# Two 1 KB loads moved from ScalarE's DMA queue into SyncE's, behind the first weight

## The chip, the cores and the metric

The kernel runs on one core of a Trainium2 chip. The metric is the device time of one execution in microseconds (us). Times of a kernel are given as the median of several runs; one further execution is recorded by the hardware profiler, and every duration of a single instruction or transfer below comes from that one.

## The reference

One token is decoded. `x` is a single row of 512 values. It is normalised, and two branches read the result; the output adds their product to `x`:

```
xn = layernorm(x)
s  = attention(xn)      # 32 heads, the last 4096 of 32768 cached keys and values, head size 128
g  = silu(mlp(xn))      # layernorm, w1, shift by one token, w2, residual, layernorm, w3, gelu, w4
out = x + s * g
```

Each head has its own keys and values. Per head the window is 4096 x 128 in bf16, 1 MB of keys and 1 MB of values, so 64 MB of cache are read once. `wq` (512 x 4096) and `wo` (4096 x 512) are 4 MB each, the weights of the second branch 3.2 MB (`w1` isn't loaded, because with one token the shift by a token leaves zeros before `w2`). Each byte is used about once: the kernel mostly moves memory.

## The kernel before

**Loads.** All large loads go through one helper, `load` (L77-78), which issues them from SyncE (SP) in the order of the program. In that order: `w2_sb` (512 KB, L86), `w3_sb` (1376 KB, L88), `w4_sb` in three pieces (L90-92), `wq_sb` (4096 KB, L94), then, from the loop at L525 on, tiles of keys and values (`kv`, 2048 KB each for two heads). The profile names the first three tiles all `w_sb`. Two loads of 1 KB don't use the helper and are issued from ScalarE (ACT): `x_bf` (L81), which lays `x` out as 128 partitions x 4 values, so 128 runs of 8 bytes, and `x_row` (L84), which puts it as four rows of 128 values on partitions 0, 32, 64 and 96 of a tile that GpSimd has cleared at L83.

**Who reads x.** `x_f` (L180) copies `x_bf` to float32. From it comes the front chain: the statistics of the first layernorm (`ln_stats`, L155-176), `xn_bf`, the second layernorm with `w2`, the products with `w3` (L212) and `w4` (L223), `g_row` (L233), then the queries: `qT_ps` (L239), `q_rows` (L246) and `q_bc` (L253), which holds each pair's query on all partitions. `x_row` is read by `xn_row` (L203) and by the last addition (L614).

**The loop.** For each of 16 pairs of heads, part of the keys is multiplied with `q_bc` on VectorE (DVE) and summed (L313, L315), the rest is transposed on TensorE, copied by ACT (L329) and multiplied with the query on TensorE (L334). Softmax is done per four heads, values are applied three pairs later (`LAG`, L442 and L431), and the result goes through `wo`.

**What orders the loads.** SP waits before an issue until the buffer is free and until an earlier load that used the same completion semaphore has landed; there are eight such semaphores for the loads of SP and ACT, used in turn. Keys have six buffers (`K_BUFS`). The first four tiles of keys are issued right behind `wq_sb`. The buffers of the values lie where the weights were: the pool of weights is closed at L529-530, so the first tile of values is issued only when the last reader of the weights' pool, the products from `q_rows` at L251, is done:

```python
        kn = load_kv(k_pool, A_k_cache, s) if s < NP else None
        if s == LAG:
            wts_guard.__exit__(None, None, None)
            v_pool = ctx.enter_context(tc.tile_pool(name="v", bufs=V_BUFS))
```

The engines' own order in the loop is the order of the program (a manual schedule, L521).

Of the kernel before, what the change touches and what calls it, by code (L numbers as in the profile page):

```python
# [8 lines left out]
P = 128  # L9
# [20 lines left out]
def kernel(  # L30
# [14 lines left out]
    nc = tc.nc  # L45
# [10 lines left out]
    KC = D // P  # L56
# [20 lines left out]
    def load(dst, src):  # L77
        return tc.keep_in_program_order(nc.sync.dma_start(out=dst, in_=src))  # L78

    x_bf = small.tile([P, KC], BF16, name="x_bf")  # L80
    nc.scalar.dma_start(out=x_bf[:], in_=A_x.rearrange("a b (p c) -> p (a b c)", p=P))  # L81
    x_row = small.tile([P, P], BF16, name="x_row")
    nc.gpsimd.memset(x_row[:], 0.0)  # L83
    nc.scalar.dma_start(out=x_row[0:P:32, :], in_=A_x.rearrange("a b (j n) -> (a b j) n", j=KC))  # L84
    w2_sb = wts.tile([P, KC, D], BF16, name="w2_sb")
    load(w2_sb[:], B_w2.rearrange("(p c) n -> p c n", p=P))  # L86
    w3_sb = wts.tile([P, KC, F], BF16, name="w3_sb")
    load(w3_sb[:], B_w3.rearrange("(p c) n -> p c n", p=P))  # L88
    w4_sb = wts.tile([P, 11, D], BF16, name="w4_sb")
# [171 lines left out]
    for c in range(2):  # L261
        nc.vector.tensor_copy(
            out=few[:, c, 0:4 * NE].rearrange("p (a b) -> p a b", b=4),
            in_=ident_bf[:, 4 * NE * c:4 * NE * (c + 1)].rearrange("p (b a) -> p a b", b=4))
# [27 lines left out]
    for r in range(2):  # L292
        nc.vector.tensor_copy(out=pick_f[:, :, r, :],
                              in_=ident_bf[:, 32 * r:32 * r + 8].rearrange("p (i a) -> p i a", a=2))
# [351 lines left out]
```

## Time and profile before

| what | value |
|---|---|
| median of 5 runs | 196.59 us |
| the five runs | 195.49, 195.68, 196.59, 196.65, 196.74 us |
| the profiled execution, its own time | 195.39 us |
| span of its instructions | 193.5 us |
| bytes loaded | 78.84 MB |
| busy: DVE, PE, ACT | 145.3, 135.9, 78.9 us |

The profile is of one execution. Its span begins with the first and ends with the last recorded instruction; the 1.9 us between span and time lie outside. The page gives busy times of the engines, and the same in 40 equal slices of 4.84 us, with the share of time in which the core's 16 DMA engines were busy and the rate at which they moved bytes. A DMA is issued by an engine's sequencer (SPq, ACTq), split into packets, put into rings of the 16 DMA engines, and lands some time later. A row of the timeline gives start, duration, engine and line of an instruction; a row of the windows gives the work of each engine, the DMA share and the rate in a stretch of time. The page's queue q1 is SP's, q10 is ACT's.

### The profile page before, as it was taken

The numbers are of one execution on the slowest core, as the hardware profiler recorded it, in microseconds if no ns is written. First come the engines' busy times: TensorE is split into PE (matmuls) and PEld (weight loads), VectorE is DVE, ScalarE is ACT, GpSimd is POOL, SyncE is SP. The second block draws the span as 40 slices with busy tenths as digits, with TensorE's granted clock in tenths as the row PEclk, the third lists the DMA queues.
The fourth block names the chain that finished last, engine by engine and source line by source line (L and its number), as shares of the span: only waits on it lengthen the run. The fifth ranks groups of instructions, "written<-read, shape, count | busy, mean of one in ns | idle before, by whom it ended". The sixth has DMA issues, their size and how long they took to land.

```text
span 193.5 us, 4727 instructions
## 1 busy us (share of the span) xinstructions
PE 135.9 (70%) x2108; PEld 104.8 (54%) x2108; DVE 145.3 (75%) x164; ACT 78.9 (41%) x173; POOL 6.3 (3%) x13
## 2 busy tenths in 40 slices
PE   0549779673785999397979976456757897857751
PEld 0444468573784945235978352146747556845640
DVE  1550119999999999999999999199999987792001
ACT  2003019871945742327468053161545047733000
POOL 2210007000000000000000000000000000000000
PEclk9999966967558559759655596995556697585555
DMA  5999999999999999999999999999999999999980
GB/s 211 404 490 433 389 423 430 428 427 433 430 427 427 423 422 423 430 433 433 430 433 420 423 433 430 430 430 430 430 430 430 430 422 435 417 433 420 410 315 5
DMA packets 7051, 79.13 MB, mean 409 GB/s; under 512 B 888, under 2 KB 1752, under 8 KB 2264
## 3 DMA queue, kind: packets, MB, share of 16 engines
q1 hardware_dynamic: 6880, 78.84, 96.0%
q8 instruction: 16, 0.26, 0.5%
q10 hardware_dynamic: 152, 0.00, 0.0%
q14 instruction: 3, 0.02, 0.0%
HBM read 78.84 MB, written 0.00 MB: 407 GB/s over the span
## 4 chain that ended last, share of the span: by engine, by line
DMA 41%; DVE 38%; PE 10%; issue 4%; SPq 3%; ACT 2%; POOL 1%; DVEq 0%; POOLq 0%
DMA kv<-in_A_k_cache_dram 31%; DVE S L315 23%; DVE prod L313 12%; DMA wo_rows<-in_A_wo_dram 7%; SPq L78 3%; DMA x_bf<-in_A_x_dram 2%; ACT kt L329 2%; PE qT_ps L239 2%; PE oT L442 2%; PE hr_ps L223 2%; PE a_ps L212 1%; PE hr_ps L220 1%; PE oT L449 1%; PE pt L328 1%; DVE m L353 1%
## 5 line engine op out<-in xcount | busy, mean ns | idle before, releaser
L315 DVE TENSOR_REDUCE S<-prod 128x20 f32<-128x2560 bf16 (+1 forms) x32 | 83.8, 2620 | 1.1
L329 ACT COPY kt<-pt 128x1024 bf16<-128x1024 bf16 x54 | 51.0, 1022 | 27.9 <-PE pt L328 27.9
L313 DVE TENSOR_TENSOR prod<-kv,q_bc 128x2560 bf16<-128x2560 bf16 (+1 forms) x32 | 44.3, 1385 | 9.2 <-DMA kv<-in_A_k_cache_dram 6.7
L328 PE MATMUL pt<-ident_bf,kv 128*128 128x128 bf16 x432 | 40.9, 277 | 10.1 <-DMA kv<-in_A_k_cache_dram 8.4
L328 PEld LDWEIGHTS <-kv 128*128 128x128 bf16 x432 | 37.3, 129 | 13.4 <-DMA kv<-in_A_k_cache_dram 9.4
L334 PE MATMUL sT<-qT_bf,kt 128*128 128x2 bf16 x432 | 17.6, 165 | 12.2 <-ACT kt L329 11.8
L442 PE MATMUL oT<-pT,kv 128*128 128x2 bf16 x768 | 22.3, 165 | 4.3 <-DMA kv<-in_A_v_cache_dram 4.3
L442 PEld LDWEIGHTS <-kv 128*128 128x128 bf16 x768 | 21.4, 102 | 5.7 <-DMA kv<-in_A_v_cache_dram 5.6
L334 PEld LDWEIGHTS <-kt 128*128 128x128 bf16 x432 | 15.6, 101 | 15.1 <-ACT kt L329 14.4
L431 PE MATMUL ov<-kv,pT 128*8 128x512 bf16 x64 | 21.9, 519 | 0.0
L431 PEld LDWEIGHTS <-pT 128*8 128x8 bf16 x64 | 6.7, 109 | 14.2 <-issue 11.5
L371 PE MATMUL mb_ps<-md,par_t 4*128 4x4 f32 x16 | 4.5, 349 | 10.1 <-DVE md L363 10.1
L378 ACT ACTIVATE pT<-S,mb 128x64 bf16<-128x64 f32 x32 | 10.9, 356 | 0.2
L371 PEld LDWEIGHTS mb_ps<-md,par_t 4*128 4x128 f32 x16 | 4.0, 306 | 10.7 <-issue 9.5
L374 ACT COPY mb<-mb_ps 128x4 f32<-128x4 f32 x8 | 1.3, 162 | 20.6 <-PE mb_ps L371 20.6
L462 DVE TENSOR_TENSOR o<-oT,rden 128x2 bf16<-128x2 f32 x3 | 0.5, 160 | 10.8 <-PE oT L442 10.8
L466 ACT ACTIVATE o<-oT,rden 128x1 bf16<-128x1 f32 x26 | 4.7, 264 | 6.3 <-PE oT L449 4.2
L226 DVE COPY hr<-hr_ps 1x512 f32<-1x512 f32 x1 | 0.7, 679 | 7.7 <-PE hr_ps L223 7.7
L378 ACT ACTIVATION_READ_ACCUMULATOR pT<-S,mb 128x1 f32 x32 | 6.0, 187 | 0.0
L157 PE MATMUL ln_ps<-x_f,ones_f 128*128 128x4 f32 x4 | 1.2, 366 | 5.8 <-DVE x_f L180 4.8
L215 ACT ACTIVATE a_bf<-a_ps 128x10 bf16<-128x10 f32 x1 | 0.2, 179 | 12.1 <-PE a_ps L212 12.1
L507 PE MATMUL yr_ps<-wo,ox 128*1 128x512 bf16 x16 | 5.0, 483 | 0.0
(116 smaller groups left out, 93.6 us busy)
## 6 DMA issues: line engine op xcount, KB each, us to landing
kv<-in_A_k_cache_dram SPq DMA_DIRECT2D x16, 2048.0 KB, 29.7
kv<-in_A_v_cache_dram SPq DMA_DIRECT2D x15, 2048.0 KB, 26.6
wq_sb<-in_A_wq_dram SPq DMA_DIRECT2D x1, 4096.0 KB, 17.8
wo<-in_A_wo_dram SPq DMA_DIRECT2D x1, 2048.0 KB, 27.1
w_sb<-in_B_w_dram SPq DMA_DIRECT2D x1, 1376.0 KB, 6.8
w_sb<-in_B_w_dram SPq DMA_DIRECT2D x1, 1024.0 KB
wo<-in_A_wo_dram SPq DMA_DIRECT2D x1, 1024.0 KB, 26.9
kv<-in_A_v_cache_dram SPq DMA_DIRECT2D x1, 1024.0 KB
```

What stands on the lines that cost most here:

```text
L78: return tc.keep_in_program_order(nc.sync.dma_start(out=dst, in_=src))
L313: nc.vector.tensor_tensor(out=prod[:, 0:m, :], in0=kn[:, rows, :], in1=q_bc[:, s:s + 1, :].to_broadcast([P, m, Dh]), op=ALU.mult)
L315: nc.vector.tensor_reduce(out=st[s // 2]["S"][:, s % 2, rows], in_=prod[:, 0:m, :], axis=AX.X, op=ALU.add)
L328: nc.tensor.transpose(pt[:, i, :], kn[:, n + b + i, :], ident_bf[:])
L329: nc.scalar.copy(out=kts[s][:, b:b + w, :], in_=pt[:, 0:w, :])
L334: nc.tensor.matmul(st[s // 2]["sT"][:, s % 2, c, :], lhsT=kt[:, c, :], rhs=qT_bf[:, 2 * s:2 * s + 2], start=True, stop=True)
L371: nc.tensor.matmul(mb_ps[:], lhsT=par_t[:].rearrange("k b a -> k (b a)"), rhs=md[:].rearrange("k r a -> k (r a)"), start=True, stop=True)
L378: nc.scalar.activation(out=s["pT"][:, i // 2, :, i % 2], in_=s["S"][:, i // 2, :], func=ACT.Exp, scale=scale, bias=mb[:, i:i + 1], accum_o ...
L431: nc.tensor.matmul(s["ov"][32 * r:32 * r + 8], lhsT=s["pT"][:, r, c:c + 4, :].rearrange("p i a -> p (i a)"), rhs=v[:, c:c + 4, :], start=F ...
L442: nc.tensor.matmul(s["oT"][:, 2 * r:2 * r + 2], lhsT=v[:, c, :], rhs=s["pT"][:, r, c, :], start=(c == 0), stop=(c == CP - 1))
L466: nc.scalar.mul(o_blk[b][:, c + k:c + k + 1], st[g]["oT"][:, hl + k:hl + k + 1], st[g]["rden"][:, hl + k:hl + k + 1])
L507: nc.tensor.matmul(yr_ps[:], lhsT=ox_blk[i][:, t:t + 1], rhs=wo_blk[i][:, t, :], start=(t == 0), stop=(t == n - 1))
```

## The change

Both loads of `x` are issued through `load`, so from SP, after `w2_sb` and ahead of `w3_sb`. The clearing of `x_row` on GpSimd stays where it was. Nothing else is edited.

```diff
     x_bf = small.tile([P, KC], BF16, name="x_bf")
-    nc.scalar.dma_start(out=x_bf[:], in_=A_x.rearrange("a b (p c) -> p (a b c)", p=P))
     x_row = small.tile([P, P], BF16, name="x_row")
     nc.gpsimd.memset(x_row[:], 0.0)
-    nc.scalar.dma_start(out=x_row[0:P:32, :], in_=A_x.rearrange("a b (j n) -> (a b j) n", j=KC))
     w2_sb = wts.tile([P, KC, D], BF16, name="w2_sb")
     load(w2_sb[:], B_w2.rearrange("(p c) n -> p c n", p=P))
+    load(x_bf[:], A_x.rearrange("a b (p c) -> p (a b c)", p=P))
+    load(x_row[0:P:32, :], A_x.rearrange("a b (j n) -> (a b j) n", j=KC))
     w3_sb = wts.tile([P, KC, F], BF16, name="w3_sb")
     load(w3_sb[:], B_w3.rearrange("(p c) n -> p c n", p=P))
```

## The prediction

> **What bounds the kernel now.** I read the page's slices and its table of queues first.
>
> ```profile
> span 193.5 us, 4727 instructions
> ...
> DMA  5999999999999999999999999999999999999980
> GB/s 211 404 490 433 389 423 430 428 427 433 430 427 427 423 422 423 430 433 433 430 433 420 423 433 430 430 430 430 430 430 430 430 422 435 417 433 420 410 315 5
> ...
> q1 hardware_dynamic: 6880, 78.84, 96.0%
> ...
> q10 hardware_dynamic: 152, 0.00, 0.0%
> ```
>
> From the second slice to the 38th the 16 DMA engines are busy nine tenths or more, at about 430 GB/s. SP's queue holds 96.0% of the engines' time. 78.84 MB at 430 GB/s are 183.4 us of the 193.5; the other 10 us are the start (nothing moves before 1.5 us, and the first slice runs at 211 GB/s) and the tail behind the last data. DVE with 145.3 us is not the bound. The chain of waits names keys with 31% and DVE with 35%, but its pieces of keys are transfers that wait in a full queue: one issued at 94.76 takes 31.37 us for 2 MB, which alone would be 4.9 us. So the time is: when the stream starts, plus 183 us, plus gaps, plus the tail. A change to two 1 KB loads can act on the start, or by letting the stream run dry later.
>
> The start, in the windows (us, five engines' busy time with counts, PE clock, DMA share, GB/s):
>
> ```profile
> 1.50:1.75 0.25, 0.00 (x0) 0.00 (x0) 0.00 (x0) 0.00 (x0) 0.25 (x2) 1.00 0.05 16
> 1.75:2.00 0.25, 0.00 (x0) 0.00 (x0) 0.00 (x0) 0.00 (x0) 0.04 (x1) 1.00 1.10 246
> 2.00:2.25 0.25, 0.00 (x0) 0.00 (x0) 0.00 (x0) 0.00 (x0) 0.00 (x0) 1.00 0.46 82
> 2.25:2.50 0.25, 0.00 (x0) 0.00 (x0) 0.00 (x0) 0.22 (x1) 0.00 (x0) 1.00 0.37 98
> 2.50:2.75 0.25, 0.00 (x0) 0.00 (x0) 0.00 (x0) 0.25 (x1) 0.00 (x0) 1.00 0.28 115
> 2.75:3.00 0.25, 0.00 (x0) 0.00 (x0) 0.00 (x0) 0.25 (x1) 0.00 (x0) 1.00 0.58 230
> 3.00:3.25 0.25, 0.00 (x0) 0.00 (x0) 0.00 (x0) 0.25 (x1) 0.00 (x0) 1.00 1.10 410
> ```
>
> The first packets of `w2_sb` move at about 1.6 us, then the engines are half empty until 2.9 us. The packet records show `w2_sb` (4096-byte packets) from 1.60 to 3.84 us, the 8-byte packets of `x_bf` between them from 2.58 to 3.86, the first of `w3_sb` (11008 bytes) at 3.63, and the four 256-byte packets of `x_row` only at 5.49 to 5.92.
>
> Then the timeline of the issues:
>
> ```profile
> 0.73 0.41 ACTq L81 DMA_DIRECT2D x_bf<-in_A_x_dram  x1
> ...
> 1.18 1.07 ACTq L84 DMA_DIRECT2D x_row<-in_A_x_dram  x1
> ...
> 3.25 0.43 SPq L78 DMA_DIRECT2D wq_sb<-in_A_wq_dram  x1
> 4.55 3.96 SPq L78 DMA_DIRECT2D kv<-in_A_k_cache_dram  x4
> 4.55 0.17 DVE L180 CAST x_f<-x_bf 128x4 f32<-128x4 bf16 x1 [3.29 <-DMA x_bf<-in_A_x_dram]
> ...
> 29.51 0.54 SPq L78 DMA_DIRECT2D kv<-in_A_v_cache_dram  x1
> ```
>
> SP issues `w2_sb` at 0.72, `w3_sb` at 1.19 and the pieces of `w4_sb` from 1.64. ACT issues x at the same time. `x_bf` lands at 4.53, and the front chain starts from it; at its end the first values are issued, at 29.51.
>
> **What the Trainium skill says.** The page "DMA: Bandwidth & Descriptors", section "Issuing engines are not separate DMA queues": DMAs of all issuers end on the same 16 engines, and issuing from several saves only sequencer time. The trace agrees: 8-byte packets of q10 lie between 4096-byte packets of q1. Same page, "Queues, rings and completion order": each engine takes the packets of one ring in order and goes round the rings of different issuers. So x, once in SP's ring, goes behind all of `w2_sb` and ahead of all of `w3_sb`; the trace of before shows the alternation. Same page, "Why a DMA increments its semaphore by 16 and not by 1": a DMA over four rows uses four engines only, and the sequencer itself writes the rest of the count. The trace has four packets for `x_row`, and an issue of 1.07 us against 0.41 for `x_bf`; whether those writes are the difference no row shows.
>
> **The change part by part.**
>
> *ACT loses two issues* (0.41 + 1.07 us). ACT's first work is a table load at 2.28 us, its first operation waits until 15.64 for PE. Worth nothing; cover is 12 us.
>
> *SP gains two issues between `w2_sb` and `w3_sb`.* `x_bf`: 0.41 us as on ACT, 0.46 with the gap to the next. `x_row`: a four-row transfer issued by SP is the store of the result at 190.37, 0.60 us; ACT's took 1.07. I take 0.60, 0.65 with the gap. So `w3_sb` is issued at 1.19 + 0.46 + 0.65 = 2.30 instead of 1.19 (2.77 with ACT's price). `x_row` also waits on SP for GpSimd's clearing, from 0.72 to 0.92, done before SP comes to it at 1.65. Behind it everything SP issues moves by 1.11 us: three pieces of `w4_sb`, `wq_sb` (3.25 to 4.36), the keys.
>
> *Does the stream notice?* `w2_sb` moved its first packet 1.60 - 0.72 = 0.88 us after its issue began. `w3_sb` could then begin at 2.30 + 0.88 = 3.18 (3.65 with ACT's price). Before, it began at 3.63, when `w2_sb` was through. So the delay hides behind `w2_sb`; without that cover it would cost 1.1 us. Lower bound: -0.45 (3.18 against 3.63), if `w2_sb` gets through sooner. Upper bound in the rival below. The next cover is larger: `w3_sb` is 1.41 MB, 3.3 us at 430 GB/s, against issues 0.5 us apart, and `wq_sb`, 4.36 + 0.88 = 5.24, is not needed before some 10 us (3.35 MB of weights at 430 GB/s after 1.6 us, with the slow start).
>
> *The packets of x* now lie in the same rings: eight of 8 bytes on each engine, recorded at 7 to 9 ns. 8 x 9 = 0.07 us between `w2_sb` and `w3_sb`. Before they went between packets of `w2_sb` and lengthened that by about the same. Bounds 0 and, if each small packet costs ten times its record, 0.7 us. I take +0.1.
>
> *When x lands.* Its last packet follows the last of `w2_sb`, 3.84 + 0.07 = 3.91 us; before it ended at 3.86 and landed 0.67 later. So 4.6 instead of 4.53. The front chain moves by +0.1 (bounds -0.5, if `w2_sb` is through sooner, and +2). Behind the chain's end wait the values, at 29.51. What lies in the queue then: issued are 3264 KB of weights, 4096 of `wq_sb`, 4 x 2048 of keys, 15.9 MB; moved are 4.84 us x (211 + 404 + 490 + 433 + 389 + 423) GB/s = 11.4 MB by 29.0 and 0.2 more, so 4.3 MB or 10 us are left. A chain 0.1 or 2 us later takes from these 10 us and costs nothing. The same count gives 8.7 us as the smallest remainder later, at 172.27, with over 10 before all others that DVE or PE release.
>
> *The completion semaphores.* `x_bf`, `x_row`, `w2_sb` used the first three of the eight in this order; now `w2_sb`, `x_bf`, `x_row` do. The first three tiles of keys wait for these loads (issues at 4.55, 5.25, 6.83). With all three landed by about 7 us as before, the keys are issued at most 1 to 2 us later, with 16 us of queue ahead of the first (6.7 MB at 4.55). Nothing.
>
> The sum: -0.1 to +0.1 at the start and 0 elsewhere; I take +0.1. The profiled execution would go from 195.39 to 195.5, the median from 196.59 to 196.7; the profiled run lay at the lower end of the five.
>
> **The rivals.**
>
> *Slower: `x_row` holds up SP's ring.* `x_row` took until 5.49 to move its first packet, 3.2 us after its issue ended, with nothing but `x_bf` ahead of it in ACT's queue. If that is a property of this small four-row transfer and not of the traffic that it met, then in SP's ring `w3_sb` stands behind it. Price: issued from 1.65 to 2.25, plus 3.2 is 5.5; `w3_sb` would begin 1.9 us later than 3.63, with nothing else in the rings. It decides by over 0.5% once `w3_sb` starts after 4.6 us. +1.0 to +2.0: 197.6 to 198.6. For it speaks the 3.2 us; against it, that `w3_sb` and the pieces of `w4_sb` were being fed to the engines at that time, which explains it as well.
>
> *Faster: the half-empty start goes.* From 1.6 to 3.6 us 0.52 MB moved where 0.86 would fit at full rate: 0.8 us. The engines lacked packets just while ACT's two issues ran beside SP's. If those caused it, `w2_sb` is through at about 2.9, and `w3_sb`, ready at 3.2, starts 0.45 us sooner; all of it would be 0.8. With the spread of the runs (two of five lie 1 us below the median) that gives 195.0 to 195.8, at best 0.8%. Against it speaks that the first packets are also slow in themselves (200 to 500 ns against 159 later).
>
> *No effect of the change as such*: the built order of instructions shows the two loads on SP where the diff puts them, so this has no share of its own.
>
> **How the numbers follow.** 0.5% (about what a measurement of this kernel can tell from no change) is 0.98 us. Likeliest, 0.44: the start moves by -0.4 to +0.5, median 196.2 to 197.1, my number 196.7; 0.02 of it falls outside 0.5% on each side by scatter. Slower rival, 0.30, of which 0.26 beyond 0.5%. Faster rival, 0.26, of which 0.22 beyond, by the spread named. So faster 0.24, same 0.48, slower 0.28. Both outer cases hold much, so the range reaches into both: 195.2 to 198.3, leaving about 0.1 out on each side.
>
> **What would show it.** In the changed kernel's windows: `w3_sb`'s rate begins without an empty stretch after `w2_sb` (right), an empty stretch after 3.5 us (slower rival), or 400 GB/s already by 2.5 us (faster rival). `x_f` should start at 4.6, `wq_sb` be issued near 4.4, the first values near 29.6. The slices from the second on should stay at 430. The prediction is wrong if the stream runs dry later, or if its steady rate depends on how it began.

## The result, and the profile after

The changed kernel takes 196.16 us (median of 44 runs, 195.42 to 197.66), the kernel before 195.49 us (79 runs taken beside them). The ratio is 1.0026, 95% interval 1.0014 to 1.0037: a loss of about 0.5 us, small, but clear of zero. The runs of the kernel before lie in two groups, three quarters at 195.3 to 195.8 us and the rest at 196.5 to 197.2, which is why its first five had the median 196.59. Because of such groups the ratios, here and below, lie near those of the mean times (195.78 and 196.28 us here) and not of the medians; runs more than 1.5% above the fastest of their kernel are left out of them, which are five of the 22 of experiment 12 and no others.

The execution profiled with this result was the longest of the 44 (197.66 us), so the changed kernel was profiled once more (195.88 us, near its median). From that second page:

```profile
span 194.0 us, 4727 instructions
...
DMA  5999999999999999999999999999999999999980
GB/s 154 417 443 432 419 426 429 424 419 432 432 429 429 426 431 429 432 429 432 429 422 426 432 426 429 429 432 432 422 429 426 432 422 429 424 434 423 411 325 15
...
q1 hardware_dynamic: 7032, 78.85, 96.2%
```

SP's queue has the 152 packets of x more than before, and q10 is gone. The middle still runs at 430 GB/s. The first slice is slower (154 against 211), and the last two still move more (325 and 15 against 315 and 5): the stream ends later. From the timeline of SP, first the store of the result in the kernel before, then the changed kernel:

```profile
190.37 0.60 SPq L78 DMA_DIRECT2D out_dram<-out_row  x1
```

```profile
1.18 0.41 SPq L78 DMA_DIRECT2D x_bf<-in_A_x_dram  x1
1.64 0.70 SPq L78 DMA_DIRECT2D x_row<-in_A_x_dram  x1
2.38 1.92 SPq L78 DMA_DIRECT2D w_sb<-in_B_w_dram  x4
4.34 0.76 SPq L78 DMA_DIRECT2D wq_sb<-in_A_wq_dram  x1
...
191.27 0.60 SPq L78 DMA_DIRECT2D out_dram<-out_row  x1
```

`w3_sb`, the first of the four `w_sb`, is issued at 2.38 instead of 1.19, and the result is stored at 191.27 instead of 190.37. So the store is 0.90 us later, but the span only 0.5 longer: from that issue to the end it takes 2.74 us instead of 3.16. There is a loss of 0.9 at the front and a gain of 0.42 at the back.

**The front**, in windows (the last two columns are DMA share and GB/s). Before:

```profile
2.75:3.25 0.50, 0.00 (x0) 0.00 (x0) 0.00 (x0) 0.50 (x1) 0.00 (x0) 1.00 0.84 320
3.25:3.75 0.50, 0.00 (x0) 0.00 (x0) 0.00 (x0) 0.32 (x1) 0.00 (x0) 1.00 0.99 386
3.75:4.25 0.50, 0.00 (x0) 0.00 (x0) 0.00 (x0) 0.00 (x0) 0.00 (x0) 1.00 1.25 485
4.25:4.75 0.50, 0.00 (x0) 0.00 (x0) 0.17 (x1) 0.00 (x0) 0.00 (x0) 1.00 1.05 396
```

Changed:

```profile
2.75:3.25 0.50, 0.00 (x0) 0.00 (x0) 0.00 (x0) 0.00 (x0) 0.00 (x0) 1.00 1.09 418
3.25:3.75 0.50, 0.00 (x0) 0.00 (x0) 0.00 (x0) 0.00 (x0) 0.00 (x0) 1.00 0.65 156
3.75:4.25 0.50, 0.00 (x0) 0.00 (x0) 0.00 (x0) 0.00 (x0) 0.00 (x0) 1.00 1.19 221
4.25:4.75 0.50, 0.27 (x2) 0.27 (x2) 0.17 (x1) 0.00 (x0) 0.00 (x0) 1.00 0.39 133
```

Up to 3.25 us the changed kernel is ahead: by then it has moved 0.46 MB, the kernel before 0.30. In the next 1.5 us it moves 0.25 MB, the kernel before 0.63. At 4.75 us 0.22 MB are missing, which is 0.5 us at 430 GB/s on the average of the engines. But the engines don't lose alike. The packet records don't name the engine; following the packets from one's end to the next one's start, all engines start `w3_sb` between 3.77 and 4.01 us in the kernel before; in the changed one ten start at 3.71 to 4.08 and six at 4.47 to 4.90. The last of them is 0.9 us later than before, and so is the store. (In the 197.66 us execution eight start by 3.76, the others from 4.39 to 5.35. Packet times here are on the page's clock; those in the prediction lie 0.15 us too early.)

**The back.** SP's semaphore instructions at the end (count, then ns min/median/max), before and changed:

```profile
L641 SPq EVENT_SEMAPHORE  x8: 17/28/953, 191.0 to 193.5; - x8
```

```profile
L641 SPq EVENT_SEMAPHORE  x8: 17/28/534, 191.9 to 193.9; - x8
```

The longest is SP's wait for the last store to land. It isn't the store that became faster (its packets lie equally far behind its issue). SP's recorded instructions show a pause of 0.46 us in which nothing is recorded, in both profiles after SP's 79th instruction. In the kernel before, that place comes behind this wait. With two more instructions on SP ahead of it, it comes in front of the wait and passes while the store is under way anyway.

### The profile page after: what moved, and what is told of

Read it like the earlier page. It is cut to its first block, busy times and chain, and to the rows that moved or that the text cites. A ratio compares the mean times of both kernels' runs of the same rounds, so it can differ in the third digit from the quotient of the medians.

```text
span 195.9 us, 4727 instructions
## 1 busy us (share of the span) xinstructions
PE 139.4 (71%) x2108; PEld 106.6 (54%) x2108; DVE 145.4 (74%) x164; ACT 79.0 (40%) x173; POOL 6.2 (3%) x13
## 4 chain that ended last, share of the span: by engine, by line
DMA 44%; DVE 29%; PE 16%; ACT 5%; SPq 3%; issue 1%; POOL 1%; POOLq 0%
DVE S L315 18%; DMA kv<-in_A_v_cache_dram 15%; DMA kv<-in_A_k_cache_dram 12%; DMA wq_sb<-in_A_wq_dram 10%; DVE prod L313 9%; DMA wo_rows<-in_A_wo_dram 7%; PE ov L431 6%; ACT kt L329 4%; PE yr_ps L507 3%; PE oT L442 3%; SPq L78 3%; PE qT_ps L239 2%; PE pt L328 1%; PE mb_ps L371 1%; ACT q_bc L253 1%
## 5 line engine op out<-in xcount | busy, mean ns | idle before, releaser
L328 PE MATMUL pt<-ident_bf,kv 128*128 128x128 bf16 x432 | 41.4, 278 | 10.3 <-DMA kv<-in_A_k_cache_dram 8.6
L334 PEld LDWEIGHTS <-kt 128*128 128x128 bf16 x432 | 16.2, 104 | 13.9 <-ACT kt L329 13.2
L374 ACT COPY mb<-mb_ps 128x4 f32<-128x4 f32 x8 | 1.3, 163 | 20.3 <-PE mb_ps L371 20.3
L507 PE MATMUL yr_ps<-wo,ox 128*1 128x512 bf16 x16 | 6.1, 562 | 0.0
L359 PE MATMUL mt_ps<-ident_f,m 128*2 128x128 f32 x8 | 2.8, 349 | 3.8 <-DVE m L353 3.8
```

Of the source, the lines that this page charges most:

```text
L328: nc.tensor.transpose(pt[:, i, :], kn[:, n + b + i, :], ident_bf[:])
L334: nc.tensor.matmul(st[s // 2]["sT"][:, s % 2, c, :], lhsT=kt[:, c, :], rhs=qT_bf[:, 2 * s:2 * s + 2], start=True, stop=True)
L507: nc.tensor.matmul(yr_ps[:], lhsT=ox_blk[i][:, t:t + 1], rhs=wo_blk[i][:, t, :], start=(t == 0), stop=(t == n - 1))
```

## The experiments

Theories at the outset: A, `w3_sb` comes too late and the rings run empty; B, the 8-byte packets in SP's ring cost; C, the four-row `x_row` holds the engines that it uses. D and T, on the back, came later. Medians are in us, ratios are to the kernel before on the same chip, with the 95% interval.

**1. The changed kernel again.** No edit.

> The changed kernel once more, for a second profile. Both theories: 195.9 to 196.4 us, ratio 1.002 to 1.004. Theory A (late w3): w3_sb is issued at 2.4 us, its first packets come when the rings have nothing else, and the rate falls near 0 for some 0.3 us around 4 us, in this profile as well. Theory B (small packets): the loss need not be at that place.

195.93, ratio 1.0021 (1.0004 to 1.0037). The profile is the one above: the place is as A expects (in quarters of a microsecond, 88 and 44 GB/s from 4.0 to 4.5 us).

**2. Only x_bf moved; 3. only x_row moved.** Each keeps the other load on ACT (the line that goes from ACT isn't shown; `...` stands for arguments that stay):

```diff
 # 2: x_bf
     load(w2_sb[:], ...)
+    load(x_bf[:], ...)
     load(w3_sb[:], ...)
 # 3: x_row
     load(w2_sb[:], ...)
+    load(x_row[0:P:32, :], ...)
     load(w3_sb[:], ...)
```

> Only x_bf moves behind w2_sb on SP, x_row stays on ACT. Theory A (what costs is that w3_sb is issued 1.2 us later and the rings run empty before it): w3_sb is issued at about 1.64, no empty stretch, 195.3 to 195.6 us, ratio 1.000. Theory B (the 128 small packets in SP's rings disturb what follows): all but a little of the loss, 196.0 to 196.2 us. Theory C (the four-row load x_row holds its four DMA engines): 195.5 us.

> Only x_row moves, x_bf stays on ACT. Theory A: w3_sb is issued at about 1.9, little or no empty stretch, 195.4 to 195.7 us. Theory B: 195.5 us, since the small packets are on the other queue. Theory C: four of the engines start w3_sb late, 196.0 to 196.2 us.

x_bf alone: 197.73, ratio 1.0088 (1.0056 to 1.0121), worse than both together and outside all three expectations. x_row alone: 195.52, 1.0011 (0.9990 to 1.0032). C falls by the profile rather than by this interval: all engines start `w3_sb` at 4.10 to 4.54 us, and no four of them stay behind. In this profile thirteen of the engines start `w2_sb` only at 2.81 to 3.08 us (all by 2.09 in 1), so that it lasts until 4.53 and covers an issue of `w3_sb` at 1.94; so 3 says little on what the later issue alone costs. A as first stated falls too, since with x_bf alone `w3_sb` is issued at 1.64, early enough by my reckoning; yet eleven engines start it at 3.25 to 3.99 us and five at 5.25 to 5.89.

**4. Both behind `w3_sb`.**

```diff
     load(w2_sb[:], ...)
-    load(x_bf[:], ...)
-    load(x_row[0:P:32, :], ...)
     load(w3_sb[:], ...)
+    load(x_bf[:], ...)
+    load(x_row[0:P:32, :], ...)
```

> Both loads on SP, but behind w3_sb, which covers 3.3 us of issues. x_bf lands at about 7.5 us, three later, within the 10 us of queue. Theory A: no empty stretch, and no second issuer at the start: 195.1 to 195.5 us. Theories B and C: 196.0 to 196.2 us, as the small packets and the four-row load still lie in SP's rings ahead of w4_sb.

194.86, ratio 0.9961 (0.9946 to 0.9976), faster than the kernel before and than the changed one. The windows of its profile have no gap:

```profile
3.25:3.75 0.50, 0.00 (x0) 0.00 (x0) 0.00 (x0) 0.00 (x0) 0.00 (x0) 1.00 1.20 497
3.75:4.25 0.50, 0.00 (x0) 0.00 (x0) 0.00 (x0) 0.00 (x0) 0.00 (x0) 1.00 1.05 440
4.25:4.75 0.50, 0.00 (x0) 0.00 (x0) 0.00 (x0) 0.00 (x0) 0.00 (x0) 1.00 1.07 440
```

All engines start `w3_sb` between 3.29 and 3.71. The store is issued at 190.40, as before (190.37); the gain is the shorter back. x lands 3.3 us later than before, and nothing comes of it.

**5. Few small packets; 6. `w3_sb` late without small packets.** 5 is the changed kernel with one 8-byte packet per engine instead of eight, 6 is kernel 4 with `w3_sb` made to wait.

```diff
 # 5
+    nc.vector.memset(x_bf[:], 0.0)
-    load(x_bf[:], ...)
+    load(x_bf[0:16, :], ...[0:16, :])
 # 6
+    nc.gpsimd.memset(w3_sb[:].rearrange("p c n -> p (c n)")[:, 0:1640], 0.0)
     load(w3_sb[:], ...)
     load(x_bf[:], ...)
     load(x_row[0:P:32, :], ...)
```

> The changed kernel, but x_bf loads only 16 of its 128 partitions: one 8-byte packet for each DMA engine instead of eight; the other 112 rows of x_bf are zeros, so the layernorm and the queries come from a part of x. The issues on SP keep their times. Theory A (w3_sb is issued too late): as the changed kernel, 195.9 to 196.2 us, with few engines busy at 3.5 to 4.5 us. Theory B (eight 8-byte packets per engine starve the rings): that loss of 0.9 us goes, the shorter end stays: 195.0 to 195.3 us.

> Both loads of x behind w3_sb, which here waits for GpSimd to clear a part of its tile, until about 2.3 us; so w3_sb is as late as in the changed kernel, with no small packets between it and w2_sb. Theory A: 195.7 to 196.0 us, w3_sb late by as much as in the changed kernel. Theory B: 194.8 to 195.2 us, little above the kernel with both loads behind w3_sb.

5: 196.24, ratio 1.0036 (1.0024 to 1.0048). 6: 196.41, ratio 1.0072 (1.0041 to 1.0103), `w3_sb` issued at 2.36. B falls as the cause of this loss: an eighth of the packets costs the same, and no packets at all, with the same late issue, no less. In 6 the windows look like those of the changed kernel:

```profile
3.25:3.75 0.50, 0.00 (x0) 0.00 (x0) 0.00 (x0) 0.00 (x0) 0.00 (x1) 1.00 1.04 247
3.75:4.25 0.50, 0.00 (x0) 0.00 (x0) 0.00 (x0) 0.00 (x0) 0.00 (x0) 1.00 0.59 110
4.25:4.75 0.50, 0.00 (x0) 0.00 (x0) 0.00 (x0) 0.00 (x0) 0.00 (x0) 1.00 0.67 220
```

**7. x_row back on ACT, x_bf behind `w3_sb`; 8. both behind `w4_sb`.**

```diff
 # 7, against 4
-    load(x_row[0:P:32, :], ...)
+    nc.scalar.dma_start(out=x_row[0:P:32, :], ...)
 # 8, against 4: the two loads of x after the third piece of w4_sb
     load(w4_sb[0:96, 10, :], ...)
+    load(x_bf[:], ...)
+    load(x_row[0:P:32, :], ...)
```

> x_bf behind w3_sb on SP, x_row on ACT. Theory D (a kernel that issues no DMA from ACT ends 0.42 us sooner, the wait of 0.95 us on SP at the end being 0.53): 195.2 to 195.4 us, the long wait is back. Without D: 194.8 to 195.0 us, as with both behind w3_sb on SP.

> Both loads of x behind all three pieces of w4_sb on SP. The front chain starts at about 11 us, 6 later, within the 10 us of queue. Theory B (small packets cost where little is queued behind them, and wq_sb is queued here): 194.6 to 194.9 us. If a small packet costs the same anywhere: 195.6 to 196.1. If the front chain's delay counts: over 196.

7: 195.97, ratio 1.0024 (1.0004 to 1.0044), runs from 195.24 to 197.28. 8: 195.59, ratio 1.0014 (0.9995 to 1.0033), its runs half at 195.0 to 195.3 and half from 195.9 up. Both missed on the whole. 8 refutes D: without a DMA on ACT its back is 3.17 us. Its SP records one instruction fewer than 4, which led to T: what counts is where SP's pause falls. x lands at 11.2 us there, and the store is issued at 190.07, the earliest so far: the front chain's delay costs nothing in this profile.

**9. Two spare loads late on SP.** The kernel before, with

```diff
         kn = load_kv(k_pool, A_k_cache, s) if s < NP else None
+        if s in (9, 10):
+            load(spare[4 * (s - 9):4 * (s - 8), :], A_x.rearrange("a b (j n) -> (a b j) n", j=KC))
```

(`spare` is a tile of 8 x 128 that nothing reads.)

> The kernel before, with two spare 1 KB loads added on SP in the loop (at the tenth and eleventh pair), into a tile that nobody reads; the start and ACT's loads are as before. Theory T (at a fixed place in SP's instruction stream, after its 79th recorded instruction, SP pauses for 0.46 us, and two more instructions ahead of it put that pause in front of the wait for the last store, where it is hidden): 195.0 to 195.2 us, 0.42 less than before, the end from the last store's issue 2.74 us instead of 3.16. If the shorter end comes from ACT issuing no DMA: 195.4 to 195.6.

195.10, ratio 0.9979 (0.9965 to 0.9994). The store is issued at 190.41, as before, and the back is 2.73. By its place the pause now lies ahead of the store's issue, where SP waits 12.8 us for the result anyway, so that it can't be told apart from that wait. T holds here, and ACT, which issues its two DMAs as before, isn't the cause.

**10. `w2_sb` and `w3_sb` exchanged; 11. x_bf behind `w2_sb`, x_row behind `w3_sb`; 12. a smaller clearing than in 6.**

```diff
 # 10, against the changed kernel
-    load(w2_sb[:], ...)
+    load(w3_sb[:], ...)
     load(x_bf[:], ...)
     load(x_row[0:P:32, :], ...)
-    load(w3_sb[:], ...)
+    load(w2_sb[:], ...)
 # 11, against 4
     load(w2_sb[:], ...)
+    load(x_bf[:], ...)
     load(w3_sb[:], ...)
-    load(x_bf[:], ...)
 # 12, against 6
-    ...[:, 0:1640], 0.0)
+    ...[:, 0:860], 0.0)
```

> The changed kernel with w2_sb and w3_sb exchanged: the first load is w3_sb (1376 KB), behind it both loads of x, then w2_sb. Theory A (the load behind x is issued 1.2 us later, its first packets come slowly, and 512 KB don't cover that): 3.3 us of w3_sb cover it, 194.7 to 195.2 us, slowest engine done with wq_sb at about 20.5 us. If small packets near the head of SP's rings cost in themselves: 195.7 to 196.2.

> x_bf behind w2_sb and x_row behind w3_sb, both on SP: w3_sb is issued at 1.64 as in the kernel with x_bf alone moved, but ACT issues nothing. Theory A alone: w3_sb is 0.45 us later than with both loads behind it, 194.8 to 195.4 us. If the 128 small packets ahead of w3_sb cost besides: 195.8 to 197. If the bad result of x_bf alone came from x_row being issued by ACT at the same time: 194.8 to 195.4.

> Both loads of x behind w3_sb, and w3_sb held by a smaller clearing until about 1.65 us (instead of 2.3 or 1.19). Theory A: w3_sb's first packets may be ready at 2.5 to 3.5 us, about when w2_sb ends: 194.9 to 195.5 us, between 194.86 (not held) and 196.41 (held to 2.3).

10: 195.38, ratio 0.9995 (0.9978 to 1.0012), over the 195.2 that A allowed. Its back is the short one, so without any loss at the front it would take 195.49 - 0.42 = 195.07; some 0.3 us of loss remain. In its profile (195.86 us) the rate falls to 90 and 205 GB/s in the two halves of 5.75 to 6.75 us, where x passes between `w3_sb` and `w2_sb`. 11: 197.66, 1.0093 (1.0061 to 1.0126). 12: 197.55, 1.0082 (1.0060 to 1.0103), with `w3_sb` issued at 1.71. All three missed A's numbers. With x_bf's packets ahead, an issue at 1.63 or 1.64 (2, 11) is worse than one at 2.4 (1, 5), clear of the intervals; without them the intervals of 12 and 6 overlap, and only the median of 12 is higher, against 7 runs of 6. In the profile of 12 fourteen engines start `w3_sb` at 3.26 to 3.84 and two at 5.69. Those two, 2 us late, set the time of this execution: its store is issued at 192.63, 2.3 us later than in the kernel before.

**13. As late as in 6, but covered; 14. the change behind 1.5 MB.** In both the 1 MB piece of `w4_sb` goes right behind `w2_sb`; 13 then holds `w3_sb` as 6 does, with x behind `w4_sb`, 14 is otherwise the changed kernel.

```diff
     load(w2_sb[:], ...)
+    load(w4_sb[:, 0:8, :], ...)
 # 13 only
+    nc.gpsimd.memset(w3_sb[:].rearrange("p c n -> p (c n)")[:, 0:1640], 0.0)
     ...
     load(w3_sb[:], ...)
-    load(w4_sb[:, 0:8, :], ...)
```

> w2_sb, then the first 1 MB of w4_sb, then w3_sb held by the clearing until about 2.3 us, the rest of w4_sb, then both loads of x. Theory A' (it is not the late issue that costs, but that engines have nothing left in SP's ring when it comes; such an engine goes on 0.8 to 2 us after the others and stays behind): w2_sb and the 1 MB last until 5.4 us, so no engine runs out: 194.8 to 195.3 us, as with x behind w4_sb without the wait, all engines starting w3_sb within 0.5 us. If the late issue as such costs: 196.0 to 196.6.

> The changed kernel with 1 MB of w4_sb loaded right behind w2_sb, ahead of x: so x stands behind 1.5 MB instead of 0.5, and w3_sb, issued at about 2.85 us, behind x. Theory A': the rings hold data until 5.4 us, 194.7 to 195.2 us. If small packets in SP's ring ahead of w3_sb cost in themselves: 195.6 to 196.4.

13: 195.27, ratio 0.9990 (0.9979 to 1.0001), with the long back of 3.17; `w3_sb` is issued at 2.36 as in 6, but the store at 190.19 instead of 191.90. The windows of 13:

```profile
3.25:3.75 0.50, 0.02 (x1) 0.00 (x0) 0.50 (x2) 0.00 (x0) 0.00 (x0) 1.00 1.06 426
3.75:4.25 0.50, 0.00 (x0) 0.00 (x0) 0.50 (x4) 0.00 (x0) 0.00 (x0) 1.00 1.01 426
4.25:4.75 0.50, 0.00 (x0) 0.00 (x0) 0.50 (x5) 0.00 (x0) 0.00 (x0) 1.00 1.00 410
```

14: 194.89, ratio 0.9975 (0.9963 to 0.9987), as good as 4. So the same two loads, ahead of the same `w3_sb`, cost little or nothing in the runs when 1.5 MB stand in front of them. A is right in this form: the late issue costs only where too little data is queued ahead of it. That the ring of a late engine is empty meanwhile isn't shown. In 2 eight of the 128 packets of x_bf, issued at 1.19, moved only at 5.24 to 5.68, just ahead of the late engines' `w3_sb`; so there something issued long before stood still too.

**15. Kernel 8 with one spare load**, as in 9, at the tenth pair.

```diff
+        if s == 9:
+            load(spare[:], A_x.rearrange("a b (j n) -> (a b j) n", j=KC))
```

> Both loads of x behind w4_sb, and one spare 1 KB load on SP in the loop, which shifts SP's pause of 0.46 us to before the wait for the last store. Theory T: 0.42 less than the same without the spare load (whose lower runs were 195.0 to 195.3): lower runs at 194.6 to 194.9, end 2.74 us after the last store's issue instead of 3.17. Without T: unchanged.

195.48, ratio 1.0007 (0.9993 to 1.0021), a back of 3.24: missed. Here the spare load also shifts which semaphore the last store uses, and SP waits for it with its 79th instruction, directly ahead of the pause. So T's place is right, but what counts is the order of pause and wait, not the number of instructions alone. (That the semaphore has shifted is inferred from the place of the wait.)

**All profiles together.** Columns: issue of `w3_sb`; end of the last packet of `wq_sb`, that is, when the slowest engine has it; issue of the last store; their difference; from that issue to the end (the back).

```
                          w3 issued  wq done   store   diff   back
before                       1.19     20.69   190.37  169.7   3.16
changed, first               2.37     23.43   193.14  169.7   2.75
1  changed, second           2.38     21.50   191.27  169.8   2.74
2  x_bf alone                1.64     23.01   193.02  170.0   3.17
3  x_row alone               1.94     20.85   190.69  169.8   3.15
4  behind w3                 1.19     20.66   190.40  169.7   2.74
5  few packets               2.37     22.02   191.73  169.7   2.74
6  held                      2.36     22.44   191.90  169.5   2.74
7  x_row on ACT              1.19     22.02   191.81  169.8   3.18
8  behind w4                 1.19     20.32   190.07  169.8   3.17
9  spare loads               1.19     20.58   190.41  169.8   2.73
10 w3 first                    -      21.39   191.26  169.9   2.73
11 bf behind w2              1.63     23.58   193.34  169.8   2.74
12 held less                 1.71     23.00   192.63  169.6   2.75
13 held, covered             2.36     20.57   190.19  169.6   3.17
14 behind w2 and w4          2.86     21.04   190.92  169.9   2.74
15 w4, spare                 1.19     20.46   190.00  169.5   3.24
```

The difference lies between 169.5 and 170.0 in all seventeen, while `wq_sb` ends anywhere from 20.3 to 23.6 us. To within 0.3 us, what the slowest engine has lost in the first 20 us is neither made good nor made worse in the other 170.

## Why the prediction was right and wrong, point by point

- **The bound** was right: the stream's start, its length and a tail set the time. It was read too coarsely. The Trainium skill, "DMA: Bandwidth & Descriptors", section "Why a DMA increments its semaphore by 16 and not by 1", says a load has landed only when all engines it uses have finished; and "Two DMAs through the same engine are not ordered" says that nothing orders DMAs across the 16 engines. The packets and the table agree: the engines start `w3_sb` up to 1.2 us apart, and the store follows the slowest one's end of `wq_sb` by 169.5 to 170.0 us.
- **ACT's two issues, worth nothing**: right for ACT itself, but x_bf on ACT slowed `w2_sb`, issued beside it. In the three profiles with x_bf there (before, 3, 9) 0.16 to 0.30 MB have moved by 3.25 us, in the other fourteen 0.37 to 0.49, also where only x_row is on ACT (2, 7).
- **SP's issues**: `w3_sb` at 2.30 (2.37 and 2.38), `wq_sb` at 4.36 (4.23 and 4.34). Right; `x_row` took 0.70 instead of 0.60.
- **"So the delay hides behind `w2_sb`"** is the step that failed. I set the first packet of `w3_sb` against the last of `w2_sb`, one time each for 16 engines. (That both are 0.15 us too early leaves the margin as it was.) But an earlier end of `w2_sb`, which I counted as a gain, also shortens the cover: its last packet ended at 3.70 us instead of 3.99. The first packet of `w3_sb` did come in time, at 3.50 and 3.71 us; but only eight or ten engines went on with it, and the others stood until 4.39 to 5.35. Measured, the step costs 0.9 us in the profile near the median and 2.8 in the longest execution, not -0.45 to +0.1. Experiments 6 and 13, and the changed kernel and 14, show that it is the cover that was too small: about as late an issue of `w3_sb` costs with 0.5 MB in front of it and not with 1.5 MB.
- **The packets of x, +0.1 us**: with an eighth of those of x_bf the time is the same (5), so nothing speaks against 0.1. They are not always free: in the profiles of 4, 10 and 14, where they lie in the rings behind other data, only some 13, 12 and 10 of the 16 engines are busy for half a microsecond when they pass; in 8 no such dip shows.
- **When x lands, and the 10 us of cover behind it**: right. `x_f` started at 4.25 (I said 4.6); in 4 and 8 it started at 7.87 and 11.21, and the store was issued at 190.40 and 190.07, no later for it.
- **The completion semaphores, nothing**: right for the keys. I counted what SP waits for, and not that its instructions stand in another place.
- **The tail** was taken as fixed. It became 0.42 us shorter, which hides nearly half of the loss. 0.90 - 0.42 = 0.48 us is what the profiles differ by, and the ratio says 0.5. That the measured 196.16 us lies near the forecast 196.7, even below it, is luck: a gain that I didn't see took off part of the loss, and I started from a median of five runs that was 1.1 us above that of 79.
- **The slower rival** had its sign right (the empty stretch after 3.5 us) and its cause wrong: x_row alone costs nothing clear, and its packets move at 4.17 to 4.35 us, right behind `w2_sb` (3). **The faster rival** was partly right. With ACT's issues gone, `w2_sb` starts without the half-empty stretch (4: 377 GB/s from 2.75 us, 320 before), and the store can come 0.3 us sooner (8), but in 4 what the start gains is gone by the store, and on the way the rate falls to 233 GB/s (6.75 to 7.25 us) where the packets of x pass.

Open: why some engines go on 0.6 to 2 us after the others. It isn't the start of a load as such: in 1 all engines begin `w2_sb` 1.02 to 1.37 us after its issue, but six begin `w3_sb` only 2.1 to 2.5 us after its own. Open is also why an issue at 1.63 to 1.71 us (2, 11, 12) leaves single engines further behind than one at 2.4 (they start `w3_sb` at 5.42 to 5.89 us at the latest, against 4.81 to 5.35); with the same 1.02 us its first packets would be there at about 2.7, well before `w2_sb` ends (the last packets at 3.67 to 3.83), so that by this estimate the rings don't run empty at all. Open too are the reason of SP's pause, the wide scatter in 7, where x_row on ACT ran beside SP's first issues and three engines fell behind within `w3_sb`, and the two groups of runs of 8 and of the kernel before. None of the runs shows what a late engine does meanwhile.

## What to carry to other kernels

At the start of a kernel that its loads bound, judge each DMA engine and not the queue: before anything small or slow is issued, queue enough data that every engine stays busy until the next large load is there, because here the slowest engine's delay stayed to the end. In this kernel 512 KB in front of two small loads were too little and 1.5 MB enough; behind the second weight the kernel even gains 0.4%, most of it at its end. And look for a change of a few tenths at the other end as well: here a shift by two instructions moved a fixed pause from behind a wait to in front of it.

## What the runs showed of the hardware that was not expected

- SP pauses for about 0.46 us at a fixed place of its instruction stream, after the 79th recorded instruction, in 16 of the 17 profiles; in the other (9) a wait covers the place. Whether that falls before or after the wait for the last store is worth 0.42 us.
- The cost of a late issue doesn't grow with its delay. With x_bf's packets ahead of `w3_sb`, an issue at 1.63 us has the ratio 1.0093 (11), one at 2.37 us 1.0026 (the changed kernel). With no small packets ahead, 1.19, 1.71 and 2.36 us have 0.9961, 1.0082 and 1.0072 (4, 12, 6); the last two can't be told apart.
- In 12 two engines start a load 2 us after the other fourteen (5.69 against 3.84 us at the latest), and the lag is still there at the store, 187 us later.
